# Output products of a linear-attention branch in 11 passes rather than 12, one iteration later, with other PSUM banks at two changes of pool

## The chip, the cores and the metric

The kernel runs on one core of a Trainium2 chip. The metric is device microseconds of one execution; three runs of the kernel before gave 1002.74, 1003.26 and 1003.54, median 1003.26.

## The reference

Two attentions over the same x (2048 tokens, 448 features, 16 heads of 28) are mixed by a gate per token, all in 32-bit floats:

```python
g = _sigmoid((x * gate_w).sum(-1, keepdims=True))
# A: phi = concat(softmax(pq), softmax(-pq)), pq = q @ w_phi per head
kv = einsum("bhsf,bhsd->bhfd", phi_k, v);  z = sum of phi_k over s
o  = (phi_q @ kv) / (phi_q . z + 1e-6);    a = o @ wo_A
# B: softmax(q k^T / sqrt(28)) v, then @ wo_B
return g * a + (1 - g) * b
```

## The kernel before

**Exact products.** A 32-bit product is made in three passes: every operand is a high part (rounded to the matmul's format) and a low part, and high·high, high·low and low·high are added in PSUM. The 448 features lie in four groups of 112, each as four strips of 28 rows in 32, so that 128 rows hold 112 of data. In each strip four rows are spare: row 28 carries the denominator, and the weights are zero against all four. Projections of x have 11 passes instead of 12, since x was packed so when it was loaded. The output product of branch A, `out_a` (L593), has 12: four groups times three, 128 tokens by 448 columns each, into the PSUM tile poa. Its stationary operand is oTa, its moving one woA_s.

**Order.** For TensorE (PE), VectorE (DVE), ScalarE (ACT) and GpSimd (POOL) the order of the code is the order of the engine. SyncE (SP) issues all transfers, in an order that the framework sets; an issue that waits holds up those behind it.

**The loop at L766** has 43 iterations. In the first 16 keys and values of branch A are made. After that, with y the iteration's number less 17, each one projects a tile of queries (pq, while there are any), makes features, turns them (pft, PE transposes copied out by ACT), and pushes a maximum unit `mx_unit` (L295 and after: scores of branch B in pmb and pmd, ACT's Relu into rl, two DVE reductions) between. Eight pairs of tiles go through four steps:

- even y: numerators (pn, L549), then `normalize1`: ACT copies pn to oUa, two transfers move the denominators, in four rows of oUa, into dena over 128 partitions;
- odd y: `normalize2`: DVE adds and inverts, two transfers write rda in DRAM, one broadcasts its four rows over 32 partitions each into rsa;
- even y, two pairs later: `normalize3`: DVE multiplies oUa by rsa (L430);
- odd y: `normalize4`: ACT casts the high parts into oTa (L438, two tiles), POOL subtracts for the low ones (L439, two).

`out_a(y - 10)` follows, two products a pair; `out_a2` (L601) multiplies by the gate on ACT and stores (ga to gad). Between them stand `value_b` products (pvb, 11 passes): values of branch B, copied out by ACT (L753) into vb.

**PSUM.** At q = NT + 4 (q = y + 1, NT = 16) the loop's pool closes and another opens; tiles pvb_next and poa_next are allocated ahead, so that other tiles fall on banks 2 to 7. After the loop a tail makes the remaining eight value products and the remaining maximum units, then a third pool opens (L1023) for the main loop over scores (st, L991), exponentials (p, L994), products with the values (pv, L1092) and maximum visits (pm, L332). That loop takes the larger part of the time; its qst and kst tiles are cleared by POOL ahead of it.

Of the kernel before, what the change touches and what calls it, by code (L numbers as in the profile page):

```python
# [40 lines left out]
def gated_mix_kernel(ctx, tc, xT, wqkB, wvB, wvA, wkAT, wqAT, phi, woA, woB,  # L41
# [73 lines left out]
    def run(dst, todo):  # L115
        for i, (l, r) in enumerate(todo):
            nc.tensor.matmul(dst, l, r, start=i == 0, stop=i == len(todo) - 1)  # L117
# [149 lines left out]
    rlt = ["rl", 1]  # L267

    def mx_unit():

        u = mxs["u"]
        if u == NF:
            return
        mx_fin()
        take_diffs(2)
        mxs["u"] = u + 1
        gq, r = divmod(u, 16)
        g, qb = divmod(gq, NQ)
        if gq < GM:
# [12 lines left out]
        pb, pd = ps_mx(f"pmb{u}", False), ps_mx(f"pmd{u}", True)  # L292
        for j in range(4):
            js = slice(32 * j, 32 * j + DH)
            nc.tensor.matmul((pb if j < 2 else pd)[:, j % 2, :], qc[js, qt * P:(qt + 1) * P],  # L295
                             kc[js, :], start=True, stop=True, tile_position=(32 * j, 0))
# [108 lines left out]
    def normalize1(pool, pn, nm, n):  # L405
# [4 lines left out]
        den = pool.tile([P, n, 16], F32, tag="den", name=f"den{nm}", bufs=2)  # L410
        for i in range(n):
            nc.sync.dma_start(den[:, i, :], oU[DH:P:32, i, :])
        return oU, den

    def normalize2(pool, oU, den, nm, n, eps):
# [6 lines left out]
        for k in range(n):  # L422
            nc.sync.dma_start(rd[:, k * 512:(k + 1) * 512], den[:, k, :])
        nc.sync.dma_start(rs.rearrange("p n q -> p (n q)"),
                          rd.unsqueeze(1).to_broadcast([4, 32, n * 512]))
# [7 lines left out]
    def normalize4(pool, oU, nm, n):  # L433

        oTn = []
        for k in range(n):
            oT = pool.tile([P, 2, 512], F32R, tag="oT", name=f"oT{nm}_{k}", bufs=2 * n)
            (nc.scalar.copy if n == 2 else nc.gpsimd.tensor_copy)(oT[:, 0, :], oU[:, k, :])  # L438
            nc.gpsimd.tensor_sub(oT[:, 1, :], oU[:, k, :], f32(oT[:, 0, :]))  # L439
            oTn.append(oT)  # L440
        return oTn
# [299 lines left out]
    def value_tile(i):  # L741

        pool = ctx.enter_context(tc.tile_pool(name=f"atv{i}", bufs=1, side="right", reuse_waits="tile"))
        v = pool.tile([P, NT // 2, H, 32], F32, name=f"vb{i}")
        nc.gpsimd.memset(v[:, :, :, 28:32], 0.0)
        nc.gpsimd.memset(v[:, :, :, 28:29], 1.0)
        return v
# [18 lines left out]
    for i in range(2 * NT + 11):  # L766
# [22 lines left out]
        if q == 2:  # L789
# [3 lines left out]
            KV = ta.tile([P, 512], F32, name="KV")  # L793
            kvT = kv_copy()
            early = [ta.tile([P, 2, 512], F32, tag="rl2", name=f"ve{i}", bufs=2) for i in range(2)]
# [24 lines left out]
        if q == NT + 4:  # L820
# [16 lines left out]
        if q == 3:  # L837
            kv_out(kvT)
        if 2 <= q - 1 < NT:
# [24 lines left out]
        if 0 <= y - 10 < NT:  # L864
            out_a(y - 10)
            out_a2(y - 10)
# [10 lines left out]
        if 0 <= q - NT - 2 < 5:  # L877
            value_b(q - NT + 1, (lambda i: i == 5 and mx_unit()) if q >= NT + 4 else None)
        if y >= 5 and y % 2 and tb - 2 < 8:
            num[tb - 2] = normalize2(ta, *num[tb - 2], f"a{tb - 2}", 2, True)  # L880
    ta_s.close()
# [71 lines left out]
    def score_group(sc):  # L953
# [34 lines left out]
        for (s, j), i in zip(sc, take):  # L988
            gq, kt = divmod(s, NT)
            st = bank(i, f"st{s}_{j}")  # L990
            nc.tensor.matmul(st, kst_of[(gq // NQ, kt // 4)][:, j, (kt % 4) * P:(kt % 4 + 1) * P],  # L991
# [15 lines left out]
    for t in range(8, NT):  # L1007
# [8 lines left out]
        if t in (8, 12):  # L1016
            load_k(0, t // 12)
# [67 lines left out]
    def values(s):  # L1085
        gq, kt = divmod(s, NT)
        g, qb = divmod(gq, NQ)
        if kt == 0:
# [234 lines left out]
```

## Time and profile before

| | |
|---|---|
| median of the runs | 1003.26 us |
| the profiled execution's own time | 1003.26 us |
| its span in the trace | 1001.5 us |
| TensorE clock granted | 0.999 |
| DVE busy | 659.8 us (66%) |
| ACT busy | 807.8 us (81%) |
| POOL busy | 240.0 us (24%) |

The span is what the trace covers; the profiled execution's own time is 1.76 us more. In rows of the timeline a line begins with start and duration in us, and the bracket at its end is how long the engine stood idle before it, and on whom; PEld is the loading of a matmul's stationary operand, which lies beside other matmuls.

### The profile page before, as it was taken

How to read it: one execution, taken by the hardware profiler on the slowest of the kernel's cores; microseconds unless marked ns; L12 is line 12 of the kernel's file. 1: busy time of each engine (PE TensorE's matmuls, PEld its weight loads, DVE VectorE, ACT ScalarE, POOL GpSimd, SP SyncE). 2: the span in 40 equal slices, each digit the busy share in tenths (PEclk: the TensorE clock that was granted, in tenths of full speed). 3: DMA queues.
4: the chain of work that ended last, by engine and by line, in shares of the span. 5: the costliest groups of instructions: out<-in, count | busy, mean ns of one | idle time of the engine just before them, and what ended most of it. 6: DMA issues, size and time to landing. Idle time of an engine off the chain costs nothing.

```text
span 1001.5 us, 18001 instructions
## 1 busy us (share of the span) xinstructions
PE 994.9 (99%) x6472; PEld 557.7 (56%) x6472; DVE 659.8 (66%) x1335; ACT 807.8 (81%) x1532; POOL 240.0 (24%) x222
## 2 busy tenths in 40 slices
PE   9999999999999999999999999999999999999998
PEld 8878878888777533333333333333334444455656
DVE  6467676887645588888888788888886544444202
ACT  5445555567855899999999999999999999979672
POOL 1265455678625211110120100102011011101010
PEclk9999999999999999999999999999999999999999
DMA  8977312312235832332525324443233264216231
GB/s 290 313 238 218 104 66 76 146 46 80 91 114 129 174 87 54 88 82 70 108 58 105 81 51 141 88 101 94 59 88 75 66 125 117 53 38 147 64 105 56
DMA packets 68353, 107.28 MB, mean 107 GB/s; under 512 B 18520, under 2 KB 28424, under 8 KB 68264
## 3 DMA queue, kind: packets, MB, share of 16 engines
q1 hardware_dynamic: 68264, 106.13, 39.0%
q8 instruction: 51, 0.84, 0.4%
q14 instruction: 38, 0.31, 0.1%
HBM read 73.44 MB, written 31.45 MB: 105 GB/s over the span
## 4 chain that ended last, share of the span: by engine, by line
PE 99%; DVE 0%; ACT 0%; issue 0%; POOL 0%; POOLq 0%; ACTq 0%
PE st L991 28%; PE pv L1092 25%; PE pm L332 9%; PE pqk L117 6%; PE poa L117 4%; PE pva L135 4%; PE pk L135 4%; PE pq L117 4%; PE pob L117 3%; PE pmb L295 2%; PE pvb L135 2%; PE pft L535 2%; PE pvb L117 1%; PE pqk L688 1%; PE pn L549 1%; PE pkv L489 1%
## 5 line engine op out<-in xcount | busy, mean ns | idle before, releaser
L994 ACT ACTIVATE p<-st 128x512 f32<-128x512 f32 x1020 | 527.9, 642 | 25.8 <-PE st L991 25.7
L343 DVE TENSOR_REDUCE part<-pm 128x1 f32<-128x512 f32 x450 | 287.6, 686 | 151.1 <-PE pm L332 151.1
L991 PE MATMUL st<-qst,kst 128*128 128x512 f32 x1020 | 301.3, 423 | 0.8 <-ACT vb L753 0.5
L1092 PE MATMUL pv<-p,vb 128*32 128x512 f32 x2048 | 263.6, 602 | 0.0
L991 PEld LDWEIGHTS st<-qst,kst 128*128 128x128 f32 x1020 | 168.8, 188 | 100.1 <-ACT p L994 45.0
L336 ACT ACTIVATE rl<-pm 128x512 f32<-128x512 f32 x200 | 124.7, 624 | 14.6 <-PE pm L332 13.0
L332 PEld LDWEIGHTS pm<-kc,qc 28*128 28x128 f32 x800 | 38.3, 181 | 167.7 <-issue 100.6
L430 POOL TENSOR_TENSOR oUb<-oUb,rsb 128x512 f32<-128x512 f32 x15 | 19.3, 1286 | 459.3 <-DMA rsb<-rdb 332.5
L340 DVE CUSTOM_DVE_ANT_0 rl<-pm,rl 128x512 f32<-128x512 f32 x150 | 102.2, 681 | 0.0
L332 PE MATMUL pm<-kc,qc 28*128 28x512 f32 x800 | 101.2, 495 | 0.0
L1092 PEld LDWEIGHTS pv<-p,vb 128*32 128x32 f32 x2048 | 47.4, 108 | 95.4 <-issue 88.7
L300 DVE CUSTOM_DVE_ANT_0 rl<-pmb,rl 128x512 f32<-128x512 f32 x112 | 72.1, 681 | 40.4 <-ACT rl L298 40.3
L298 ACT ACTIVATE rl<-pmd 128x1024 f32<-128x1024 f32 x56 | 57.6, 1028 | 17.0 <-PE pmd L295 9.4
L117 PE MATMUL pqk<-XH,wB 128*128 128x512 f32 x192 | 59.3, 397 | 0.0
L625 ACT CAST ev<-pqk 128x512 fp32r<-128x512 f32 x28 | 16.1, 588 | 37.9 <-PE pqk L117 28.8
L117 PE MATMUL poa<-woA_s,oTa 128*128 128x448 f32 x180 | 40.7, 375 | 0.0
L117 PEld LDWEIGHTS pqk<-XH,wB 128*128 128x128 f32 x192 | 35.4, 188 | 8.5 <-issue 1.5
L1107 DVE SCALAR_TENSOR_TENSOR acc<-pob,gate,acc 128x448 f32<-128x448 f32 x12 | 8.2, 681 | 47.1 <-PE pob L117 47.1
L135 PE MATMUL pva<-wvA_s,XH 128*128 128x450 f32 x128 | 38.6, 375 | 0.0
L135 PE MATMUL pk<-wkA_s,XH 128*128 128x448 f32 x128 | 37.5, 374 | 0.0
L626 DVE TENSOR_TENSOR ev<-pqk,ev 128x512 fp32r<-128x512 f32 x28 | 19.0, 690 | 28.0 <-ACT ev L625 27.9
L117 PE MATMUL pq<-wqA_s,XH 128*128 128x448 f32 x128 | 37.3, 374 | 0.0
(172 smaller groups left out, 1163.3 us busy)
## 6 DMA issues: line engine op xcount, KB each, us to landing
qkd<-ev SPq DMA_DIRECT2D x28, 512.0 KB
qst<-qkd SPq DMA_DIRECT2D x64, 224.0 KB
kst<-qkd SPq DMA_DIRECT2D x64, 224.0 KB
od<-oTb SPq DMA_DIRECT2D x48, 112.0 KB
rsa<-rda SPq DMA_DIRECT2D x8, 512.0 KB
rsb<-rdb SPq DMA_DIRECT2D x15, 256.0 KB
kc<-qkd SPq DMA_DIRECT2D x64, 56.0 KB
gad<-ga SPq DMA_DIRECT2D x16, 224.0 KB
```

The lines of the kernel that those rows point to most:

```text
L117: nc.tensor.matmul(dst, l, r, start=i == 0, stop=i == len(todo) - 1)
L135: nc.tensor.matmul(dst[:, :n], l, r, start=i == 0, stop=i == len(todo) - 1, skip_group_check=True)
L295: nc.tensor.matmul((pb if j < 2 else pd)[:, j % 2, :], qc[js, qt * P:(qt + 1) * P], kc[js, :], start=True, stop=True, tile_position=(32 * ...
L298: nc.scalar.activation(rl, pd, AF.Relu)
L300: nc.vector.tensor_tensor_reduce(rl[:, i, :], pb[:, i, :], rl[:, i, :], 1.0, LOWEST, ALU.add, ALU.max, part[:, col + i:col + i + 1])
L332: nc.tensor.matmul(pm[j], mxs[("qc", gq)][js, qt * P:(qt + 1) * P], mxs[("kc", g, kb)][js, :], start=True, stop=True, tile_position=(32 * ...
L336: nc.scalar.activation(rl, pm[kb], AF.Relu if kb < 3 else AF.Copy)
L340: nc.vector.tensor_tensor_reduce(r, pm[j], r, 1.0, LOWEST, ALU.add, ALU.max, part[:, col + j:col + j + 1])
L343: nc.vector.tensor_reduce(part[:, col + j:col + j + 1], pm[j], AX.X, ALU.max)
L991: nc.tensor.matmul(st, kst_of[(gq // NQ, kt // 4)][:, j, (kt % 4) * P:(kt % 4 + 1) * P], qst_of[gq][:, j, :], start=True, stop=True)
L994: nc.scalar.activation(p, st, AF.Exp, scale=SCALE)
L1092: nc.tensor.matmul(pv[32 * j:32 * j + 32, :], vb[kt // 8][:, kt % 8, 4 * g + j, :], pt[j], start=kt == 0, stop=kt == NT - 1, tile_position ...
```

## The change

**Eleven passes.** The low·high pass of the fourth group goes. Its 112 rows of the stationary operand, low parts for the pair's two tiles, are copied by four transfers per pair (`take_spread`, 28 rows to 4 spare rows times 7 slots of 256 columns, in each strip) into the spare rows of seven other passes' operands; the matching rows of the weights stand in the spare rows of the moving operands. For the low·high passes of groups 0 to 2 that takes copies of the weights: woC0, in seven strips of 64 columns that lie in unused columns of wqA_s, and woC_s. `spare_weights` loads the rows in two iterations early in the second part.

**Normalisation.** The denominators move in one transfer instead of two, the inverses in one instead of two, the broadcast in four of 32 partitions instead of one of 128. One subtraction of each pair moves from POOL to DVE. oTa is one tile a pair.

**One iteration later.** `out_a` takes y - 11, the loop has 44 iterations, five value products stand at other iterations, and one maximum unit moves from the tail into the loop (56 in all, as before). Also the rl tiles alternate between two pools near the end of the loop, and vb's ones are set later on POOL.

**PSUM.** The first change of pool comes one iteration later, without the two tiles allocated ahead: maximum units start on banks 0 to 5, others on 6 and 7. At the second change, pv0 is allocated right behind the tile st1_0.

```diff
@@ run
-            nc.tensor.matmul(dst, l, r, start=i == 0, stop=i == len(todo) - 1)
+            d = dst.rearrange("p (a n) -> p a n", n=64) if len(r.shape) == 3 else dst
+            nc.tensor.matmul(d, l, r, start=i == 0, stop=i == len(todo) - 1)
@@ mx_unit
-        rl = rlp.tile([P, 2, 512], F32, tag=rlt[0], name=f"rl{u}", bufs=rlt[1])
+        if rl_at:
+            rl_at.append(rl_at.pop(0))
+            rl = rl_at[0][0].tile([P, 2, 512], F32, tag=rl_at[0][1], name=f"rl{u}", bufs=1)
+        else:
+            rl = rlp.tile([P, 2, 512], F32, tag=rlt[0], name=f"rl{u}", bufs=rlt[1])
@@ normalize1
-        den = pool.tile([P, n, 16], F32, tag="den", name=f"den{nm}", bufs=2)
-        for i in range(n):
-            nc.sync.dma_start(den[:, i, :], oU[DH:P:32, i, :])
+        den = pool.tile([P, 16 * n], F32, tag="den", name=f"den{nm}", bufs=2)
+        nc.sync.dma_start(den, oU[DH:P:32].rearrange("p n q -> p (n q)"))
@@ normalize2
-        for k in range(n):
-            nc.sync.dma_start(rd[:, k * 512:(k + 1) * 512], den[:, k, :])
-        nc.sync.dma_start(rs.rearrange("p n q -> p (n q)"),
-                          rd.unsqueeze(1).to_broadcast([4, 32, n * 512]))
+        nc.sync.dma_start(rd, den)
+        if n == 1:
+            nc.sync.dma_start(rs[:, 0, :], rd.unsqueeze(1).to_broadcast([4, 32, 512]))
+            return oU, rs
+        for j in range(4):
+            nc.sync.dma_start(rs[32 * j:32 * j + 32].rearrange("p n q -> p (n q)"),
+                              rd[j:j + 1].to_broadcast([32, n * 512]))
@@ normalize4
-            oT = pool.tile([P, 2, 512], F32R, tag="oT", name=f"oT{nm}_{k}", bufs=2 * n)
...
-            nc.gpsimd.tensor_sub(oT[:, 1, :], oU[:, k, :], f32(oT[:, 0, :]))
+        o = pool.tile([P, n, 2, 512], F32R, tag="oT", name=f"oT{nm}", bufs=2)
...
+            (nc.vector if n == 2 and k == 0 else nc.gpsimd).tensor_sub(
+                o[:, k, 1, :], oU[:, k, :], f32(o[:, k, 0, :]))
+        if n == 2:
+            spread.append(o)
+        return [o[:, k] for k in range(n)]
+    def take_spread():
+        while spread:
+            o = f32(spread.pop())
+            for r in range(0, P, 32):
+                nc.sync.dma_start(
+                    o[r + DH:r + 32].rearrange("p k i n -> p (k i n)")[:, :1792].rearrange(
+                        "p (s n) -> p s n", n=256),
+                    o[r:r + DH, 1, 1, 256:])
+    def spare_weights(i):
+        for r in range(0, P, 32):
+            w = w_d["woA"][r:r + DH, 0, 3].rearrange("(p s) d -> p s d", s=7)
+            a, c = f32(woA_s[r + DH:r + 32, 0, :, :D]), f32(woC_s[r + DH:r + 32])
+            for d, x in (((a[:, 0:2], w[:, 0:2]), (a[:, 2:4], w[:, 4:6])) if i == 0 else
+                         ((f32(woC0[r + DH:r + 32]), w[:, 2].rearrange("p (a n) -> p a n", n=64)),
+                          (c, w[:, 3::3]))):
+                nc.sync.dma_start(d, x)
@@ out_a
-        run(po[:, :D], [x for g in range(NG)
-                        for x in out_passes(oTs[tb][g // 2], g % 2 * 256 + tl * P, woA_s[:, :, :, :D], g)])
+        todo = [x for g in range(NG)
+                for x in out_passes(oTs[tb][g // 2], g % 2 * 256 + tl * P, woA_s[:, :, :, :D], g)][:11]
+        for g in range(3):
+            todo[3 * g + 2] = todo[3 * g + 2][0], woC_s[:, g - 1, :] if g else woC0
+        run(po[:, :D], todo)
@@ the loop
-    for i in range(2 * NT + 11):
+    for i in range(2 * NT + 12):
...
+            woC_s = ta.tile([P, 2, D], F32R, name="woC_s")
+            woC0 = wqA_s.rearrange("p i b n -> p (i b) n")[:, :7, D:]
+            nc.sync.dma_start(f32(woC_s), w_d["woA"][:, 0, 1:3])
+            nc.sync.dma_start(f32(woC0), w_d["woA"][:, 0, 0].rearrange("p (a n) -> p a n", n=64))
...
-        if q == NT + 4:
+        if q == NT + 5:
...
-            pv_next.append(ps_s("pvb_next"))
-            po_next.append(ps_s("poa_next"))
         if q == NT + 8:
-            rlp, rlt[:] = ta, ("rl2", 2)
+            rl_at[:] = [(rlp, "rl"), (ta, "rl2")]
...
+            take_spread()
...
+        if q in (4, 5):
+            spare_weights(q - 4)
...
-        if 0 <= y - 10 < NT:
-            out_a(y - 10)
-            out_a2(y - 10)
+        if 0 <= y - 11 < NT:
+            out_a(y - 11)
+            out_a2(y - 11)
...
-        if 0 <= q - NT - 2 < 5:
-            value_b(q - NT + 1, (lambda i: i == 5 and mx_unit()) if q >= NT + 4 else None)
+        if q - NT in (3, 4, 6, 7, 9):
+            value_b(3 + (3, 4, 6, 7, 9).index(q - NT), (lambda i: i == 5 and mx_unit()) if q >= NT + 5 else None)
@@ scores, before the score tile's matmul
+            if (s, j) == (1, 0):
+                pv_of[0] = ps2.tile([P, 512], F32, tag="pv", name="pv0", bufs=1)
@@ set-up of the main loop
-    kst = [stack(f"kst{i}", True) for i in range(5)]
+    kst = [stack("kst0", True)]
+    value_ones(vb[1])
+    kst += [stack(f"kst{i}", True) for i in range(1, 5)]
...
+    load_k(0, 0)
```

On PE, at the first output product (names: pn numerators, pft turned features, poa output products of branch A; the figures are tile numbers), before:

```order
L549 MATMUL pn3_1_2554<-fT3_2449,KV_2053 32x256 x4
L117 MATMUL poa0_2583<-woA_s_1874,oTa0_0_2494 128x448 x6
L117 MATMUL poa0_2583<-woA_s_1874,oTa0_1_2497 128x448 x6
L535 MATMUL pft8_0_2600<-ident_76,feat0_464 128x128 x4
L535 MATMUL pft8_4_2601<-ident_76,feat0_464 128x128 x4
```

and of the change, at the same place, and then where the product stands now:

```order
L568 MATMUL pn3_0_2578<-fT3_2469,KV_2053 32x256 x4
L568 MATMUL pn3_1_2579<-fT3_2469,KV_2053 32x256 x4
L554 MATMUL pft8_0_2608<-ident_76,feat0_464 128x128 x4
L554 MATMUL pft8_4_2609<-ident_76,feat0_464 128x128 x4
L118 MATMUL pq12_2620<-wqA_s_665,XH_89 128x448 x2
```

```order
L554 MATMUL pft9_0_2663<-ident_76,feat1_465 128x128 x4
L554 MATMUL pft9_4_2664<-ident_76,feat1_465 128x128 x4
L118 MATMUL poa0_2675<-woA_s_1874,oTa0_2514 128x448 x2
L118 MATMUL poa0_2675<-wqA_s_665,oTa0_2514 128x448
L118 MATMUL poa0_2675<-woA_s_1874,oTa0_2514 128x448 x2
L118 MATMUL poa0_2675<-woC_s_2054,oTa0_2514 128x448
L118 MATMUL poa0_2675<-woA_s_1874,oTa0_2514 128x448 x2
L118 MATMUL poa0_2675<-woC_s_2054,oTa0_2514 128x448
L118 MATMUL poa0_2675<-woA_s_1874,oTa0_2514 128x448 x2
```

The product poa0 has gone from behind the fourth pair's numerators to behind the next turn, and in the third, sixth and ninth place it reads wqA_s and woC_s; it has eleven passes.

On SP, around the broadcast of the fifth pair (rsa4), before, with what each issue waits for in brackets (DMAHW and a number is an earlier transfer's end):

```order
L602 DMA gad0_69<-ga3_2840 128x448 [waits DMAHW3_49,Activation_49]
L423 DMA rda4_2845<-dena4_2737 4x32x16 [waits DMAHW4_49,DVE_49]
L423 DMA rda4_2845<-dena4_2737 4x32x16 [waits DMAHW5_49]
L424 DMA rsa4_2846<-rda4_2845 128x1x1024 [waits DMAHW6_49,DMAHW5_49,DMAHW4_49]
L412 DMA dena5_2903<-oUa5_2900 128x1x16 [waits DMAHW7_49,Activation_49]
L412 DMA dena5_2903<-oUa5_2900 128x1x16 [waits DMAHW0_49,Activation_49]
L602 DMA gad1_70<-ga4_2925 128x448 [waits DMAHW1_49,Activation_49]
L602 DMA gad1_70<-ga5_2987 128x448 [waits DMAHW2_49,Activation_49]
```

and of the change:

```order
L635 DMA gad0_69<-ga3_2937 128x448 [waits DMAHW2_49,Activation_49]
L457 DMA oTa3_2963<-oTa3_2963 4x7x256 [waits DMAHW3_49,DVE_49,Pool_49]
L431 DMA rsa4_2858<-rda4_2857 32x1024 [waits DMAHW4_49,DMAHW0_49]
L431 DMA rsa4_2858<-rda4_2857 32x1024 [waits DMAHW5_49]
L431 DMA rsa4_2858<-rda4_2857 32x1024 [waits DMAHW6_49]
L431 DMA rsa4_2858<-rda4_2857 32x1024 [waits DMAHW7_49]
L457 DMA oTa3_2963<-oTa3_2963 4x7x256
L457 DMA oTa3_2963<-oTa3_2963 4x7x256 [waits DMAHW1_49]
L457 DMA oTa3_2963<-oTa3_2963 4x7x256 [waits DMAHW2_49]
L635 DMA gad1_70<-ga4_3001 128x448 [waits DMAHW3_49,Activation_49]
```

The broadcast is four issues now and stands behind the first of the four spread transfers of the fourth pair (oTa3), whose wait for DVE and POOL is ahead of it; the other three follow it.

On PE, at the first change of PSUM (pvb and pvb_next value products of branch B, pmb and pmd the maximum unit), before:

```order
L117 MATMUL pvb4_3192<-wvB_s_1875,XL_90 128x448
L117 MATMUL pvb4_3192<-wvB_s_1875,XH_89 128x448 x2
L295 MATMUL pmb37_3211<-kp0_1_520,qp2_0_1524 128x512 x2
L295 MATMUL pmd37_3212<-kp0_1_520,qp2_0_1524 128x512 x2
L117 MATMUL poa_next_3210<-woA_s_1874,oTa4_0_3073 128x448 x6
L117 MATMUL poa_next_3210<-woA_s_1874,oTa4_1_3076 128x448 x6
```

and of the change:

```order
L118 MATMUL pvb4_3242<-wvB_s_1875,XL_90 128x448
L118 MATMUL pvb4_3242<-wvB_s_1875,XH_89 128x448 x2
L296 MATMUL pmb38_3268<-kp0_1_520,qp2_0_1524 128x512 x2
L296 MATMUL pmd38_3269<-kp0_1_520,qp2_0_1524 128x512 x2
L118 MATMUL poa9_3279<-woA_s_1874,oTa4_3087 128x448 x2
L118 MATMUL poa9_3279<-wqA_s_665,oTa4_3087 128x448
L118 MATMUL poa9_3279<-woA_s_1874,oTa4_3087 128x448 x2
L118 MATMUL poa9_3279<-woC_s_2054,oTa4_3087 128x448
L118 MATMUL poa9_3279<-woA_s_1874,oTa4_3087 128x448 x2
L118 MATMUL poa9_3279<-woC_s_2054,oTa4_3087 128x448
L118 MATMUL poa9_3279<-woA_s_1874,oTa4_3087 128x448 x2
L296 MATMUL pmb39_3294<-kp0_1_520,qp2_0_1524 128x512 x2
```

Before, the first unit on new banks is pmb37, behind the value product pvb4 and ahead of poa_next; now it is pmb38, in the same place, and poa9 and another unit follow.

More of the change, by code (lines that the diff above doesn't have):

```diff
@@ L433, in normalize4 @@
     def normalize4(pool, oU, nm, n):
-        oTn = []
+        o = pool.tile([P, n, 2, 512], F32R, tag="oT", name=f"oT{nm}", bufs=2)
         for k in range(n):
-            oT = pool.tile([P, 2, 512], F32R, tag="oT", name=f"oT{nm}_{k}", bufs=2 * n)
[L438 to L441, printed above, removed]
+            (nc.scalar.copy if n == 2 else nc.gpsimd.tensor_copy)(o[:, k, 0, :], oU[:, k, :])
+            (nc.vector if n == 2 and k == 0 else nc.gpsimd).tensor_sub(
[3 more added lines that the diff above has]
+        return [o[:, k] for k in range(n)]
+    spread = []
+    def take_spread():
[6 more added lines that the diff above has]
+                    o[r:r + DH, 1, 1, 256:])
     def out_passes(oT, c, w, g):
@@ L793, in gated_mix_kernel @@
             KV = ta.tile([P, 512], F32, name="KV")
+            woC_s = ta.tile([P, 2, D], F32R, name="woC_s")
+            woC0 = wqA_s.rearrange("p i b n -> p (i b) n")[:, :7, D:]
+            nc.sync.dma_start(f32(woC_s), w_d["woA"][:, 0, 1:3])
+            nc.sync.dma_start(f32(woC0), w_d["woA"][:, 0, 0].rearrange("p (a n) -> p a n", n=64))
             kvT = kv_copy()
-            early = [ta.tile([P, 2, 512], F32, tag="rl2", name=f"ve{i}", bufs=2) for i in range(2)]
+            early = [ta.tile([P, 2 - i, 512], F32, tag=f"rl{i + 2}", name=f"ve{i}", bufs=1) for i in range(2)]
             early = [e.rearrange("p t (h d) -> p t h d", d=32) for e in early]
@@ L1015, in gated_mix_kernel @@
         take_acts()
-        if t in (8, 12):
-            load_k(0, t // 12)
+        if t == 12:
+            load_k(0, 1)
     while mxs["u"] < NF:
@@ L1087, in values @@
         g, qb = divmod(gq, NQ)
-        if kt == 0:
+        if kt == 0 and gq:
             pv_of[gq] = ps2.tile([P, 512], F32, tag="pv", name=f"pv{gq}", bufs=1)
```

8 lines of the change are left out of this document (6 added, 2 removed).

## The prediction

> **What bounds the kernel now.** The first view is the page's head and its chain of work.
>
> ```profile
> span 1001.5 us, 18001 instructions
> ...
> PE 994.9 (99%) x6472; PEld 557.7 (56%) x6472; DVE 659.8 (66%) x1335; ACT 807.8 (81%) x1532; POOL 240.0 (24%) x222
> ...
> PE 99%; DVE 0%; ACT 0%; issue 0%; POOL 0%; POOLq 0%; ACTq 0%
> ```
>
> PE is busy for 994.9 of 1001.5 us, and 99% of the chain that ended last is PE's. So the end is set by how much PE has to do and by the few places where it stops. The second view, the waits of PE, names every one of these places; the last three columns are the total, the count and the longest.
>
> ```profile
> PE pqk L671 <- POOL ident masks.py:199: 1.4, 1, 1.4
> PE pmb L295 <- ACT vb L753: 0.6, 1, 0.6
> PE st L991 <- ACT vb L753: 0.5, 1, 0.5
> PE st L991 <- DVE acc L1107: 0.3, 1, 0.3
> ```
>
> The middle two belong to the change: each is the first matmul on PSUM banks that were handed over. Everything else that PE could gain is work taken out of its stream. So the sum has three terms: passes removed, stalls removed, and stalls added, chiefly the wait of an output product for the new spread transfers.
>
> **The passes removed.** The third view is the chain in order of time (start, duration).
>
> ```profile
> 212.02 2.23 PE pq L117 x11
> ...
> 240.93 2.66 PE poa L117 x12
> ...
> 248.16 2.46 PE poa L117 x12
> ```
>
> An output product of 12 passes takes 2.46 us where it follows work of the same form; the 2.66 of the other contains 0.2 of drain after the narrow numerator matmuls, which the change doesn't touch. That is 2.46/12 = 0.205 us a pass, and 2.23/11 = 0.203 in the projection of queries beside it. I take 0.204. Each of the 16 products loses one: 16 × 0.204 = **−3.27 us**. All of it lies on PE, which has no slack there, so it comes off the chain in full, unless PE then waits.
>
> The eleven passes that stay keep their shape (448 output columns, 128 rows). One of them per product reads its moving operand as seven strips of 64 columns from spare columns of another weight tile. No row of the trace has a moving operand in strips. Bounds: nothing, since as many elements are read in the same order, and at worst a second pass each, 16 × 0.204 = +3.3. I take nothing, by the rows nearest to it (passes from 0.203 to 0.205 whatever weight tile they read), and keep the other end as a rival. Strips that read faster than a contiguous row I exclude, so there is no gain below nothing.
>
> **The two stalls removed.**
>
> ```profile
> 279.96 0.50 PE L295 MATMUL pmb<-kp,qp 28*128 28x512 f32 x2 [0.62 <-ACT vb L753]
> ```
> ```profile
> 279.37 0.53 ACT L753 COPY vb<-pvb 128x448 f32<-128x448 f32 x1 [1.05 <-PE pvb L117]
> ```
>
> At the first change of PSUM the maximum unit follows a value product at once, and its bank is the one that ACT is just copying out: the copy runs from 279.37 to 279.90 and PE starts 0.06 later. In the order of the changed kernel the first unit after the change takes banks 0 and 1 (no longer 2 to 5), which were freed an iteration earlier; the bank of the value product just made goes to the next unit, with a 2.2 us output product in between. **−0.62 us**, and nothing is late next there: ACT's copy takes 0.53, the product ahead of the next unit 2.2.
>
> ```profile
> 335.53 0.73 PE L991 MATMUL st<-qst,kst 128*128 128x512 f32 x2 [0.48 <-ACT vb L753]
> 336.20 1.07 PE L1092 MATMUL pv<-p,vb 128*32 128x512 f32 x8
> ```
> ```profile
> 333.01 2.05 ACT L950 ACTIVATE p<-st 128x1024 f32<-128x1024 f32 x2 [0.23 <-PE st L942]
> 334.96 0.53 ACT L753 COPY vb<-pvb 128x448 f32<-128x448 f32 x1
> ```
>
> At the second change the second score tile waits for the copy of the last value product, which ends at 335.49. In the changed order the bank of that product is not among the next score tiles'; the value accumulator, allocated earlier, takes a bank whose exponential is the second of the two at 333.01, over by 335.06, before PE reaches that accumulator (at 336.20, or 335.72 without the stall). **−0.48 us**, kept only if ACT follows; see the rivals.
>
> **The stall added.** Now a product of the first tile of a pair cannot start before four spread transfers of that pair have landed. Tightest is the pair whose casts are at 259.42; its first product takes the place of the one at 267.99.
>
> ```profile
> 257.80 0.50 PE L295 MATMUL pmb<-kp,qp 28*128 28x512 f32 x2
> ...
> 267.99 2.70 PE L117 MATMUL poa<-woA_s,oTa 128*128 128x448 f32 x12
> ```
> ```profile
> 259.42 1.16 ACT L438 CAST oTa<-oUa 128x512 fp32r<-128x512 f32 x2
> ...
> 268.37 1.17 ACT L438 CAST oTa<-oUa 128x512 fp32r<-128x512 f32 x2
> ```
> ```profile
> 260.53 2.54 POOL L439 TENSOR_TENSOR oTa<-oUa,oTa 128x512 fp32r<-128x512 f32 x2
> ```
> ```profile
> 239.40 1.16 SPq L423 DMA_DIRECT2D rda<-dena  x2
> 242.02 0.55 SPq L424 DMA_DIRECT2D rsa<-rda  x1
> ```
>
> Counted from 257.80: the casts end at +2.78; POOL now makes one subtraction of 2.54/2 = 1.27, to +4.05 (the other is on DVE meanwhile); then SP issues eight transfers, because the four broadcasts of the next pair stand between the first spread and the other three. One issue takes about 0.54 (0.55 in the last row), so the eighth starts at 4.05 + 7 × 0.54 = +7.83. The product is due at 267.99 − 257.80 = 10.19, less two passes already saved, 0.41: +9.78. That leaves 1.95 us for ℓ, the time from the start of the last issue to landing. The other pairs by the same steps: 5.1, 5.9, 3.7, then this 1.95, then 2.1 plus what was waited before it, 2.65, 3.8 plus what was waited, 3.1.
>
> What is ℓ? Nearest are the two SP rows: a small transfer with a dependent one behind it. The second of the two at 239.40 starts near 239.98, and the broadcast that needs it at 242.02: 2.04 us for 8 KB. A spread moves 28 KB, from four partitions at a time. The row nearest in rate is the broadcast out of four rows (columns: stretch, length, then PE, PEld, DVE, ACT, POOL busy, clock, share of the DMA engines, GB/s):
>
> ```profile
> 210.50:215.50 5.00, 5.00 (x30) 4.66 (x29) 4.20 (x9) 2.88 (x5) 3.97 (x3) 1.00 0.25 91
> ```
>
> A share of 0.25 is 4 of 16 engines, 91 GB/s: 28.7 KB take 0.3. So ℓ ≈ 2.3 and the tightest pair waits 0.35; the others wait nothing. I take **+0.4 us**. The bounds: 0 (ℓ below 1.95) and, with ℓ = 6.8 as in a row of the slower rival below, 4.85 at this pair alone. The Trainium skill has a rule that speaks against cutting the broadcast into four ("DMA: Bandwidth & Descriptors", Rules for kernel authors: two transfers to disjoint partition halves serialize, so one should be used); the same page, under "Why a DMA increments its semaphore by 16 and not by 1", makes the number of engines a divisor of the slowest dimension, which would give 4 engines to a transfer out of 4 rows and 16 to one of 32 rows. The 0.25 above agrees with the second rule; by the first the four would last the old 5 us together and the spreads behind them would land at about 4.6 + 5.0 + 0.9 = +10.5, a wait of 0.7 rather than 0.4.
>
> **The rest costs nothing**, each for a reason. DVE takes the subtraction over:
>
> ```profile
> L626 DVE TENSOR_TENSOR ev<-pqk,ev 128x512 fp32r<-128x512 f32 x28 | 19.0, 690 | 28.0 <-ACT ev L625 27.9
> ```
> ```profile
> 261.47 1.09 DVE L469 TENSOR_REDUCE fsumq<-feat 128x32 f32<-128x896 f32 x1 [0.57 <-ACT feat L462]
> ...
> 276.90 1.23 DVE L430 TENSOR_TENSOR oUa<-oUa,rsa 128x1024 f32<-128x1024 f32 x1 [1.04 <-DMA rsa<-rda]
> ```
>
> 0.69 a pair, into waits of DVE for ACT and transfers of 0.57 to 1.04 (that cover gone, 8 × 0.69 on DVE, and PE would see it only through the maximum units). The broadcast now issues behind a spread that waits for the subtraction, so DVE's multiplication may start up to 0.6 later, inside the 1.04; behind the waiting spread stand on SP that broadcast and the gate store, which ACT needs two iterations later. SP gains five issues a pair; twelve in all are 6.5 us of the 9.0 between the two casts above. The 18 loads of weights stand some 60 us ahead of their use. The products one iteration later shift PE's work, not its amount.
>
> **Sum**, against the profiled execution, whose own time is 1003.26 (1.76 around the span), the same as the median of the runs: 1003.26 − 3.27 − 0.62 − 0.48 + 0.4 = **999.3 us**.
>
> **Rivals.**
>
> *Slower: the spreads land late.* All small transfers share one queue with stores and the broadcasts, and the trace has slow ones:
>
> ```profile
> 267.86 0.53 SPq L424 DMA_DIRECT2D rsa<-rda  x1
> ...
> 270.85 1.24 SPq L423 DMA_DIRECT2D rda<-dena  x2
> ...
> 278.27 0.55 SPq L424 DMA_DIRECT2D rsa<-rda  x1
> ```
>
> Three microseconds behind a broadcast, the second small transfer starts at 271.47 and its dependant at 278.27: up to 6.8 us. At ℓ = 3 the pairs wait 1.05 + 0.35 = 1.4 (1000.3); at 3.9 about 4.2, all that was gained; above 4.45 more than 6.4, and the kernel is over 2 us slower; at 5 it is 1.3 + 3.05 + 2.35 + 1.9 = 8.6 (1007.5). For it: this row. Against it: what held those transfers up was a broadcast confined to a quarter of the engines, which the change cuts up.
>
> *Strips cost a second pass:* 999.3 + 3.3 = 1002.6. Nothing speaks for it but that no row shows the form.
>
> *The gain isn't passed on*, since ACT is nearly as full as PE in the main loop (PE, PEld, DVE, ACT, POOL):
>
> ```profile
> 350.00:400.00 50.00, 50.00 (x313) 19.23 (x310) 40.26 (x83) 48.38 (x98) 8.43 (x8) 1.00 0.30 70
> ```
>
> 48.38 of 50 us: PE arriving earlier finds ACT with 3% of room, and the 0.48 of the second stall may come back as a wait for an exponential: 999.8. Against more than that: ACT's own inputs come earlier by as much as PE does.
>
> **Chances.** Forecast (ℓ up to 3, 998.9 to 1000.3) 0.70; larger ℓ up to 3.9 0.08; slower by late spreads 0.08; strips 0.07; gain given back at ACT 0.07. The range runs from 998.4 (no wait, with half a microsecond for what the shifted order may save) to 1002.6 (strips) and leaves out the late spreads. A measurement of this kernel can tell about 0.2%, 2 us, from no change: faster 0.70 + 0.07 + half of the 0.08 = 0.81; within 2 us 0.11; slower 0.08.
>
> **What would show it.** Eleven passes in 2.25 and 2.45 us in the chain (strips: above 2.4 and 2.6); the two waits for ACT's copy gone from PE's list; a new wait of a product for a transfer, at the fourth pair, under 1 us. Waits there of 3 us, or waits for DVE's subtraction or for exponentials right after the second change, would make this wrong.

## The result, and the profile after

The changed kernel takes 1007.38 us (median of six runs, 1006.88 to 1009.51) beside 1003.68 for the kernel before (six runs, 1002.74 to 1004.75): a ratio of 1.0039, 95% interval 1.0026 to 1.0052. It is 3.7 us slower, where 4 us faster was forecast. Later comparisons are each with runs of the kernel before on the same chip, whose median lay between 1002.58 and 1003.13.

The page of the changed kernel:

```profile
span 1005.5 us, 18087 instructions
...
PE 993.6 (99%) x6456; PEld 555.5 (55%) x6456; DVE 670.0 (67%) x1343; ACT 807.4 (80%) x1532; POOL 230.8 (23%) x214
...
PE 95%; SPq 1%; DMA 1%; DVE 1%; ACT 0%; issue 0%; POOL 0%; POOLq 0%; ACTq 0%; DVEq 0%
```

PE has sixteen matmuls fewer, as it should, and yet the span is 4.0 us longer. The chain that ended last is no longer PE's alone: SP's issues, transfers and DVE are in it. The waits of PE say where:

```profile
PE poa L118 <- DMA oTa<-oTa: 3.7, 2, 2.4
PE poa L118 <- DMA gad<-ga: 1.9, 1, 1.9
PE pqk L704 <- POOL ident masks.py:199: 1.4, 1, 1.4
PE poa L118 <- ACT rl L303: 0.6, 2, 0.4
PE st L1036 <- DVE acc L1155: 0.3, 1, 0.3
PE poa L118 <- ACT vb L790: 0.3, 1, 0.3
```

The two waits for ACT's copy at the changes of PSUM (0.62 and 0.48) are gone. In their place stand six waits of output products, 6.5 us in all. The one put down to a gate store ("gad<-ga", 1.9) is a wait for spreads too: that store was issued 0.1 us behind the last spread of its pair, and the product doesn't read what it writes. So, most likely, are those put down to ACT (0.17, 0.40 and 0.29): each of these products starts 3.5 to 3.7 us after the last spread of its pair began to be issued, as the others do (3.4 to 3.6), and without spreads (e1, below) none of the waits is there. For the 0.17 alone the end of ACT's Relu would fit as well. The chain in order of time shows the passes themselves:

```profile
238.90 2.44 PE poa L118 x11
245.91 2.24 PE poa L118 x11
```

2.24 for eleven passes, 0.204 each, against 2.46 for twelve; the strips cost nothing. At the longest stop, though, a product is slow as well. The timeline of PE, and below it the windows around that stop (PE, PEld, DVE, ACT, POOL busy, granted clock, DMA share, GB/s):

```profile
284.52 0.50 PE L296 MATMUL pmb<-kp,qp 28*128 28x512 f32 x2
...
287.39 1.09 PE L118 MATMUL poa<-woA_s,oTa 128*128 128x448 f32 x2 [2.36 <-DMA oTa<-oTa]
288.65 0.95 PE L118 MATMUL poa<-woA_s,oTa 128*128 128x448 f32 x2
```
```profile
284.90:287.00 2.10, 0.13 (x4) 0.00 (x0) 1.65 (x4) 2.10 (x4) 0.00 (x0) 1.00 0.58 186
287.00:290.50 3.50, 3.11 (x9) 2.82 (x10) 2.10 (x3) 0.20 (x1) 1.34 (x3) 0.51 0.09 33
290.50:292.00 1.50, 1.50 (x9) 1.31 (x7) 0.00 (x0) 0.64 (x1) 0.00 (x0) 1.00 0.61 188
```

After 2.36 us without work the granted clock is 0.51 for 3.5 us; the product takes 3.88 in the chain instead of 2.44 as the next one does, 1.4 us more:

```profile
287.39 3.88 PE poa L118 x11
...
294.57 2.44 PE poa L118 x11
```

So the stops cost 6.5 + 1.4 = 7.9 in this trace.

Now the pair that the prediction took for the tightest, on SP and DVE of the changed kernel:

```profile
259.93 0.64 SPq L457 DMA_DIRECT2D oTa<-oTa  x1
260.67 2.07 SPq L431 DMA_DIRECT2D rsa<-rda  x4
262.78 1.98 SPq L457 DMA_DIRECT2D oTa<-oTa  x3
264.86 0.39 SPq L635 DMA_DIRECT2D gad<-ga  x1
```
```profile
258.11 1.76 DVE L445 TENSOR_TENSOR oTa<-oUa,oTa 128x512 fp32r<-128x512 f32 x1
```
```profile
258.03 1.29 POOL L445 TENSOR_TENSOR oTa<-oUa,oTa 128x512 fp32r<-128x512 f32 x1
```
```profile
267.65 0.64 PE L118 MATMUL poa<-woA_s,oTa 128*128 128x448 f32 x2 [1.93 <-DMA gad<-ga]
```

DVE's subtraction lasts until 259.87, 0.55 behind POOL's; the eight issues start over 4.2 us; the last spread starts at 262.78 + 1.98 - 0.64 = 264.12 and its product at 267.65: a landing of 3.5 us. Here and below, landing is counted from the start of the pair's last issue to the start of the product that waited for it.

### The profile page after: what moved, and what is told of

Same layout as the page of the kernel before. It is cut to its first block, busy times and chain, and to the rows that moved or that the text cites. A ratio compares the mean times of both kernels' runs of the same rounds, so it can differ in the third digit from the quotient of the medians.

```text
span 1005.5 us, 18087 instructions
## 1 busy us (share of the span) xinstructions
PE 993.6 (99%) x6456; PEld 555.5 (55%) x6456; DVE 670.0 (67%) x1343; ACT 807.4 (80%) x1532; POOL 230.8 (23%) x214
## 4 chain that ended last, share of the span: by engine, by line
PE 95%; SPq 1%; DMA 1%; DVE 1%; ACT 0%; issue 0%; POOL 0%; POOLq 0%; ACTq 0%; DVEq 0%
PE st L1036 28%; PE pv L1140 25%; PE pm L337 9%; PE pqk L118 6%; PE pva L136 4%; PE pk L136 4%; PE pq L118 4%; PE pob L118 3%; PE pvb L136 2%; PE poa L118 2%; PE pmb L296 2%; PE pft L554 1%; PE pqk L721 1%; PE pkv L508 1%; PE poL L1178 1%; SPq L457 1%
```

## The experiments

Theory L says that the loss is PE's stops for late spread transfers, and the rest of the sum was right. Theory S, its rival, puts the loss on the strips, the shift by an iteration or the banks.

**No spread transfers** (e1).

```diff
-            take_spread()
+            spread.clear()
```

> Leaves out the four spread transfers of every pair (the spare rows then hold other data, so the low-by-high part of the fourth group is not added); the eleven passes, the shift by one iteration and the banks stay. Theory L (late spreads): PE's stops ahead of the output products 6, 8, 10 and 14 (1.93, 0.29, 2.36 and 1.31 us) and the lowered clock behind the longest (about 1.3 us) go: 1007.4 - 7.2 = about 1000.2, and PE waits for no transfer. Rival S (strips, the shift or the banks cost): those stay, and it remains above 1004.

Measured 998.12 beside 1002.58, ratio 0.9953 (0.9938 to 0.9967): 4.5 us under the kernel before, where passes and stalls alone were reckoned at 4.37. PE's list keeps two waits only:

```profile
PE pqk L704 <- POOL ident masks.py:199: 1.4, 1, 1.4
PE st L1036 <- DVE acc L1155: 0.3, 1, 0.3
```

Theory S falls. The main loop's first product with values starts at 331.32 here and at 340.27 in the change, 8.9 us later. Of these 0.34 stood already before the first spread was issued (the numerators ahead of it start at 226.40 and 226.74). The stops and the clock explain 7.9; the rest, 0.7 in small slips, is not assigned.

**Twelve passes, no spreads** (e8): also without spare weights.

```diff
-                for x in out_passes(oTs[tb][g // 2], g % 2 * 256 + tl * P, woA_s[:, :, :, :D], g)][:11]
-        for g in range(3):
-            todo[3 * g + 2] = todo[3 * g + 2][0], woC_s[:, g - 1, :] if g else woC0
+                for x in out_passes(oTs[tb][g // 2], g % 2 * 256 + tl * P, woA_s[:, :, :, :D], g)]
...
-            take_spread()
+            spread.clear()
...
-        if q in (4, 5):
-            spare_weights(q - 4)
```

> Twelve passes again, no spread transfers and no loads of spare weights; the shift by one iteration, the merged and split transfers of the normalisation, the subtraction on DVE and the banks stay. Theory L: the time of the kernel without spreads plus 16 x 0.204 = 3.3, so about 1003.5, 0.3 to 1 below the kernel before, whose two stalls at PSUM changes (0.62 and 0.48) are gone. Rival S: the shift or the banks cost something, above 1005.

1001.37 beside 1002.58, ratio 0.9987 (0.9977 to 0.9996): 1.2 us faster than the kernel before, by the two stalls at PSUM (1.1). The difference to e1, 3.25, is 16 × 0.203. This is the fastest version here that does the whole computation; it beats both kernels.

**A quarter of the bytes** (e2): each spread moves 64 of 256 columns.

```diff
-                        "p (s n) -> p s n", n=256),
-                    o[r:r + DH, 1, 1, 256:])
+                        "p (s n) -> p s n", n=256)[:, :, :64],
+                    o[r:r + DH, 1, 1, 256:320])
```

> Each spread moves 64 of its 256 columns (7 KB rather than 28; the rest of the spare rows keeps other data, so part of the low-by-high product of the fourth group is wrong). If the landing of a spread is paid by its bytes, it falls from 3.4 us after the last issue to about 2.3 and PE's stops shrink by 3 us or more (below 1004.5). If it is a fixed time (theory L's form), the landing stays above 3.0 and the time within 1 us of the change's.

998.86 in one run. The last pair's fourth spread starts at 299.84 (the first of these rows, less one issue) and the product at 301.91: landing in 2.07 us.

```profile
297.70 2.78 SPq L457 DMA_DIRECT2D oTa<-oTa  x4
```
```profile
301.91 0.64 PE L118 MATMUL poa<-woA_s,oTa 128*128 128x448 f32 x2 [0.60 <-DMA oTa<-oTa]
```

So fewer bytes go with a shorter landing. But the framework also ordered SP otherwise here, with the spreads of most pairs in one row, so that this run alone doesn't separate bytes from order.

**Both subtractions on POOL** (e4).

```diff
-            (nc.vector if n == 2 and k == 0 else nc.gpsimd).tensor_sub(
+            nc.gpsimd.tensor_sub(
```

> Both subtractions of a pair on POOL again, one after the other (2.55 us), none on DVE. In the change the two run side by side and last up to 1.7 us. Theory L: the first spread of a pair is issued about 0.7 us later, the stops of PE grow, +0.5 to +2.5 us. Rival D (the place on DVE behind two reductions is what makes the spreads late): the spreads are issued earlier, and the time falls by 1 us or more.

1008.22 in one run beside 1002.58, 5.6 over the kernel before against 3.7 for the change; stops of 9.6 us against 6.5, though no lowered clock follows any of them. The moved subtraction helps, as theory L has it; its place on DVE is not the fault.

**Stores later, from ACT** (e10): gate stores out of the way of the spreads.

```diff
-        nc.sync.dma_start(ga_d[t // 4][:, t % 4], ga)
+        ga_late.append((t, ga))
+        if t:
+            store_ga()
...
+    def store_ga():
+        t, ga = ga_late.pop(0)
+        nc.scalar.dma_start(ga_d[t // 4][:, t % 4], ga)
```

> The gate stores (224 KB, 16 engines) are issued by ACT, each one product later, instead of by SP right behind the spread transfers. Theory C (the last spread lands late because a gate store issued behind it runs on the same engines, and because stores stand ahead of spreads on SP): landing after the last issue falls from 3.4 to 3.6 us to about 2.6, the stops ahead of products 6, 10 and 14 from 1.9, 2.4 and 1.3 to about 1.1, 0.6 and 0.4, the clock is not lowered: about 1002.5, 4 to 5 us under the change. Rival O (the spread's own 28 KB out of 28 rows by four engines take that long): landing stays at 3.2 or more and the time within 1.5 us of the change's 1007.4.

1009.98 beside 1003.05, ratio 1.0056 (1.0035 to 1.0076). Three stops make 6.4 us, and the landing is 3.7 to 4.1 us: nothing gained. In the trace the clock is at half behind each of the three; the one run of the four whose mean granted clock was 1.000 took 1006.25, the others, at 0.995, 1009.63 to 1010.80. It doesn't refute theory C cleanly, since the stores came to lie among the spreads again, only from another queue:

```profile
306.08 2.80 SPq L457 DMA_DIRECT2D oTa<-oTa  x4
```
```profile
307.33 0.33 ACTq L643 DMA_DIRECT2D gad<-ga  x1
```
```profile
312.09 0.64 PE L118 MATMUL poa<-woA_s,oTa 128*128 128x448 f32 x2 [1.56 <-DMA oTa<-oTa]
```

At this last pair the fourth spread starts near 308.23, the windows show data until 310.3, and the product starts at 312.09. What holds it for the last 1.8 us no view shows.

**Casts at the end of the iteration before** (e12): the block with `normalize4` and `take_spread` stands behind `out_a2`, at even y from 8.

```diff
-        if y >= 9 and y % 2 and tb - 4 < 8:
+        if y >= 8 and y % 2 == 0 and tb - 4 < 8:
```

> The casts, subtractions and spreads of a pair stand at the end of the iteration before (behind the output product and its gate, ahead of a value product), two to four microseconds earlier. Theory L: PE's stops ahead of the output products (1.9, 0.3, 2.4, 1.3 us and the lowered clock's 1.3) go but for 0.5 us: about 1000.5 on the scale of the change's 1007.4, 2.5 to 4 us under the kernel before. Rival A: ACT's cast waits for DVE's multiplication and so for a late broadcast, holds up the score and gate copies behind it, and gives back 2 us or more (above 1002.5).

1009.58 beside 1003.05, ratio 1.0065 (1.0050 to 1.0080). No product waits for a spread any more, and it is slower still: rival A. ACT's cast now waits for DVE's multiplication, and what is queued behind it on ACT stops PE, twice with the clock at half behind the stop:

```profile
PE pft L554 <- ACT fT L557: 4.6, 2, 3.0
PE poa L118 <- ACT fT L557: 1.5, 1, 1.5
```

**Casts ahead of the maximum unit** (e3): the same block, above `mx_unit()` of its own iteration.

```diff
-        if q in (0, 1) or q >= 11:
-            mx_unit()
         if y >= 9 and y % 2 and tb - 4 < 8:
...
+        if q in (0, 1) or q >= 11:
+            mx_unit()
```

> Casts, subtractions and spreads stand ahead of the maximum unit of their iteration instead of behind it: ACT casts 1.0 us earlier, DVE subtracts ahead of its two reductions. Theory L: the first spread of a pair is issued about 1 us earlier, the stops at products 6 and 14 shrink by about 1 us each, that at 10 by less since SP still waits for a gate store there: -2 to -4 us against the change. Rival: nothing, since SP and not the subtraction sets the issue.

1003.74 in one run beside 1003.05, some 3 us better than the change. Left are a stop of 2.5 at product 6, with the lowered clock behind it, and two of 0.6 and 0.4. At product 6 four broadcasts still stand among the spreads and took 3.25 us to issue.

**One broadcast again** (e5).

```diff
...
-        for j in range(4):
-            nc.sync.dma_start(rs[32 * j:32 * j + 32].rearrange("p n q -> p (n q)"),
-                              rd[j:j + 1].to_broadcast([32, n * 512]))
+        nc.sync.dma_start(rs.rearrange("p n q -> p (n q)"),
+                          rd.unsqueeze(1).to_broadcast([4, 32, n * 512]))
```

> The broadcast is one transfer of 128 partitions out of four rows again, three issues fewer on SP. If four transfers of 32 partitions use more engines than one out of four rows, the single one lasts about 5 us at a share of 0.25 of the engines, the spreads queued behind it land 2 us or more later, and the kernel is slower than the change by 3 us or more. If they serialize anyway, it is faster by about 1 us at the pairs where a broadcast stands between the spreads (three issues of 0.45 us fewer).

1028.02 in one run beside 1003.05: 20 us slower than the change.

```profile
PE poa L118 <- DMA oTa<-oTa: 13.1, 3, 6.8
PE poa L118 <- ACT oTa L440: 4.1, 1, 4.1
PE poa L118 <- DMA dena<-oUa: 3.6, 1, 3.6
```

Here is the landing of many microseconds behind a broadcast that the prediction's slower rival feared. The split into four is what keeps it away. The Trainium skill's advice against two transfers to disjoint partitions ("DMA: Bandwidth & Descriptors", Rules for kernel authors) does not hold for a broadcast out of four rows; the same page's rule on the number of engines agrees, with a DMA share of 0.25 for the one broadcast of the kernel before and 0.91 where the four move in the changed kernel (262.50 to 263.50).

**Only the order on SP** (e14): broadcasts of the next pair ahead of all four spreads.

```diff
...
+            with tc.issue_after(rsa_last[0].ins):
                 for r in range(0, P, 32):
                     nc.sync.dma_start(
```

> Only the order on SP changes: the four broadcasts of the next pair stand ahead of the four spread transfers of this pair (in the change they stand behind the first of them). Theory Q (part of the lateness is SP's order): the last spread of the pair of casts near 257 is issued at about 262 rather than 264.1, its stop of 1.93 us goes; the pairs without broadcasts in between keep theirs (2.36 with the lowered clock, 1.3): about 2 us under the change, 1005.4. Rival F (the four engines are the limit, not the issue): the spreads land as late as before, within 0.7 us of the change.

1003.30 beside 1003.13, ratio 1.0003 (0.9993 to 1.0012): 3.5 us of the change's loss, more than the 2 that were expected. The pair of the rows above issues its spreads from 259.37 to 262.01, and its product stops for 0.46 instead of 1.93. What stays is the stop at product 10 (1.86) with the clock behind it, and one of 1.28 at product 14.

**Order and casts** (e15): e14 and e3 together.

> Casts ahead of the maximum unit and broadcasts ahead of the spreads together. Theory L with Q: stops of PE for spreads under 0.7 us in all, no lowered clock: 999 to 1000.5, 2.5 to 4 us under the kernel before. Rival F: the stop at product 6 stays at 2 us or more with the lowered clock behind it, about 1003.5 as with the casts first alone.

1002.86 beside 1003.13, ratio 0.9997 (0.9988 to 1.0006), no difference. The trace is of a run of 1004.80, one of two out of eleven that took over 1004; both had a mean granted clock of 0.998, the others 0.999 or 1.000. In it the stop at 6 is gone, but one of 1.74 appears at product 12: the last spread of that pair was issued at 292.00 and its wait ended at 296.86, with copies into vb, loads and a store beside it (DMA share about 1.0 from 294.5 on). The clock is at half behind it. Two smaller stops are 0.73, of a maximum unit for DVE, and 0.32 at product 10.

**One strip** (e16): one spread a pair instead of four.

```diff
-            for r in range(0, P, 32):
+            for r in range(96, P, 32):
```

> One spread per pair (the last strip) instead of four; the spare rows of the other strips keep other data. If a spread of 28 KB takes 3.4 us to land by itself, its landing stays at 3.2 or more after its issue. If the four queue for the same four engines (each holds them for 0.5 to 0.75 us and one is issued every 0.65), a single one lands in 2.4 to 2.8. The time falls to 998 to 999 in either case.

999.10 in one run, and no stop. The single spread of the last pair is issued at 297.79; the windows show next to nothing from 298.25 to 299, then its packets, then a store:

```profile
298.25:299.00 0.75, 0.75 (x6) 0.69 (x5) 0.73 (x4) 0.03 (x1) 0.00 (x0) 1.00 0.01 2
299.00:300.25 1.25, 1.25 (x9) 0.73 (x7) 0.00 (x0) 0.60 (x1) 0.00 (x0) 1.00 0.13 34
300.25:301.25 1.00, 1.00 (x9) 0.88 (x6) 0.00 (x0) 0.77 (x1) 0.00 (x0) 1.00 0.62 229
```

Its data moves from 1.2 to 2.5 us after issue. No product waits for it, so its landing as counted here is not measured. In e10 the windows show data until 2.1 us after the issue of the fourth spread, and the product still started 1.8 later. So this run does not show that a spread alone lands sooner than the fourth of four. The changed kernel's windows at its last pair don't either; there the spreads start at 304.50 to 306.65, a store is issued at 307.40, and the product starts at 310.26:

```profile
305.75:307.00 1.25, 1.25 (x9) 0.69 (x7) 0.00 (x0) 0.56 (x1) 0.00 (x0) 1.00 0.20 57
307.00:307.25 0.25, 0.25 (x5) 0.23 (x2) 0.00 (x0) 0.06 (x1) 0.00 (x0) 1.00 0.00 0
307.25:308.25 1.00, 1.00 (x6) 0.82 (x5) 0.00 (x1) 0.96 (x1) 0.00 (x0) 1.00 0.19 52
308.25:309.00 0.75, 0.70 (x6) 0.19 (x4) 0.75 (x3) 0.46 (x1) 0.00 (x0) 1.00 0.92 279
309.00:310.00 1.00, 0.00 (x0) 0.00 (x0) 0.56 (x2) 1.00 (x2) 0.00 (x0) 1.00 0.09 25
```

The spreads keep a fifth of the engines busy, with a gap at 307.00; the store's burst follows at 308.25, and whose data moves in the last microsecond cannot be told. Whether the last spread waits for its sisters, for the store or for neither stays open.

**Halves** (e17): e14, with four spreads of 14 KB for the pair's first tile and four for the second.

```diff
...
+                for h in range(0, 256, P):
                     for r in range(0, P, 32):
...
+                                "p (s n) -> p s n", n=256)[:, :, h:h + P],
+                            o[r:r + DH, 1, 1, 256 + h:256 + h + P])
```

> Broadcasts ahead of the spreads as before, and each spread in two of 14 KB: four for the pair's first tile, then four for its second, which is wanted an iteration later. Theory F' (the spreads of a pair queue for the same few engines, so landing goes by the bytes ahead): the first four land about 2.6 us after the last of them is issued rather than 3.4 to 3.6, the stop at product 10 falls from 1.9 to about 1 and the one at 14 below 0.5; 1001 to 1002, 1.5 to 2.5 us under the order alone (1003.3). Rival I (each issue and its landing are a fixed time): landing stays, and four more issues on SP make it 1003.5 or more.

1008.37 beside 1002.64, ratio 1.0052 (1.0036 to 1.0068). Both theories had a part: the landing does fall, to 2.5 us at product 10,

```profile
284.92 5.30 SPq L459 DMA_DIRECT2D oTa<-oTa  x8
```
```profile
289.39 0.79 PE L118 MATMUL poa<-woA_s,oTa 128*128 128x448 f32 x2 [4.29 <-DMA oTa<-oTa]
```

(the fourth of eight starts at 284.92 + 3 × 0.67 = 286.93), but eight issues hold SP for 5.3 us, and the inverses and broadcasts behind them push the next pair's spreads back. SP's row of issues is itself a limit.

**Halves and casts** (e19).

> Halved spreads, broadcasts ahead of them, and casts ahead of the maximum unit. With F' and the earlier casts the stops for spreads are below 0.5 us in all and the clock isn't lowered: 999.5 to 1001, 2 to 3.5 us under the kernel before. If the stop of 1.7 us at product 12, behind the large copies into vb, is set by those copies, it stays, with the lowered clock: about 1002.

1009.66 beside 1002.64, ratio 1.0067 (1.0054 to 1.0080); a miss for the same reason.

**Two of four on POOL** (e18, and timed again): e14, with two spreads on POOL's queue.

```diff
-                    nc.sync.dma_start(
+                    (nc.sync if r < 64 else nc.gpsimd).dma_start(
```

> Broadcasts ahead of the spreads, and two of the four spreads issued by POOL instead of SP. If issue in a row on one queue is what counts, the last of SP's is issued 1.3 us earlier and the stops at 10 and 14 shrink by about 1 us each: 1001 to 1002. If POOL takes longer to start a transfer, or all share the same engines, there is no gain: 1003 or more.

> The kernel with two of four spreads on POOL and the broadcasts ahead, timed: its one look gave 1002.34 beside 1002.64 of the kernel before. Its stops for spreads (0.7), for the maximum units and the numerators (1.5) are 2.2 us over the sum without spreads (998.1 to 998.9): 1000.5 to 1002.5.

A single run gave 1002.34; timed, 1002.80 beside 1002.76, ratio 0.9999 (0.9990 to 1.0007). The stops for spreads are down to 1.0 us, but two new ones stand at one iteration, with 3.4 us at half clock behind them (the single run has the same two without it):

```profile
259.35 0.50 PE L296 MATMUL pmd<-kp,qp 28*128 28x512 f32 x2 [0.68 <-DVE part L305]
260.62 1.16 PE L569 MATMUL pn<-fT,KV 56*32 56x256 f32 x32 [0.77 <-ACT fT L558]
```

DVE is late there because a multiplication that takes 1.16 in the change takes 3.29 beside POOL's:

```profile
254.78 3.29 DVE L437 TENSOR_TENSOR oUa<-oUa,rsa 128x1024 f32<-128x1024 f32 x1
```

**All four on POOL** (e20).

```diff
-                    nc.sync.dma_start(
+                    nc.gpsimd.dma_start(
```

> All four spreads issued by POOL, right behind its own subtraction; SP keeps stores, inverses and broadcasts only. Theory: SP's row of issues and the lateness of the broadcasts go; POOL's fourth is issued as late as SP's fourth was (0.61 each), so landing and the stops at 10 and 14 stay near 1 us; 1001 to 1003. Rival (the POOL queue uses other or more engines): no stop for a spread, below 1000.5.

1011.37 beside 1002.76, ratio 1.0083 (1.0069 to 1.0097). Stops for spreads are 3.2 us, and the multiplications on DVE now take up to 5.07.

## Why the prediction was wrong, step by step

- Passes removed (-3.27): right. Without spreads, eleven passes beat twelve by 3.25 us (e1 against e8).
- Stalls removed (-0.62 and -0.48): right. They are gone from PE's list, and e8 is 1.2 us under the kernel before.
- Strips at nothing: right, 2.24 us for eleven passes.
- The gain passed on by ACT in the main loop: right, e1 shows the whole 4.5 us at the end.
- **The stall added (+0.4): wrong by 7.5 us**, and it is the step that failed: "So ℓ ≈ 2.3 and the tightest pair waits 0.35; the others wait nothing." Measured were stops of 6.5 us at six products and 1.4 us of lowered clock. In its parts, at the tightest pair, counted from the same maximum unit (255.09 in the changed kernel): the casts ended at +2.78, as reckoned. The subtractions ended at +4.78, not +4.05. The eighth issue started at +9.03, not +7.83 (a spread takes 0.64 to issue, not 0.54). Landing took 3.5, not 2.3. That sums to 2.4 us, of which 0.35 + 2.4 less 0.85 by which the product itself was due later gives the 1.9 that was measured. At this pair the landing is the largest part. The price was taken from one small transfer with nothing behind it; the last of four of 28 KB, issued 0.65 apart, landed after 3.4 to 3.6 us, of four of 14 KB after 2.5 (e17), of four of 7 KB after 2.07 (e2). Why the larger ones take that long is open.
- The landing alone does not make the loss. With 3.5 for ℓ and the prediction's own times for the rest, the waits come to about 2.8 us; 6.5 were measured. The time that the prediction left for the landing was too long at every pair that stopped: 3.55, 3.1, 1.6, 3.2, 1.0 and 2.3 (landing less stop, at products 0, 4, 6, 8, 10 and 14), where 5.1, 3.7, 1.95, 2.1 and the 1.93 waited before it, 2.65 and 3.1 had been reckoned.
- "The others wait nothing" failed by what stands ahead on SP: at product 10 the spreads were issued 0.9 us after the subtraction, behind broadcasts, a load and a store, and stopped PE for 2.36, longer than the pair taken for the tightest.
- "DVE takes the subtraction over" at 0.69: mis-sized. The row used has one operand from PSUM; this one reads two from SBUF beside POOL, and takes up to 1.76.
- The slower rival had the right mechanism and the right side, with a chance of 0.08. It put the point of decision at ℓ = 4.45; with the later subtraction and issue and the clock, 3.5 was enough. What spoke against it (the split broadcast) was true, as e5 shows, and not sufficient. Its price at ℓ = 3.9, "all that was gained", left out the clock.

The experiments settle that the spreads are the whole loss, and that SP's order (e14) and the time of the subtraction (e4, one run) each hold a part of it; that the bytes of a spread do is supported by e17 and e2, with other things changed beside them. They do not settle what makes the landing long, the sisters of a spread or other traffic: moving the stores (e10) only moved where they meet the spreads, and at product 12 of e15 a spread with much traffic beside it landed after 4.9 us.

## What to carry to other kernels

When a change puts a transfer between two engines' work, price the whole path to its landing at the busiest place: the last of several issues on its queue, behind everything else the queue must issue, with what else is in flight. Here a slack of 2 us against a landing reckoned at 2.3 was not a small stop but the largest term. On a kernel bound by PE a stop of two microseconds can have a lowered clock behind it (1.4 us more at one stop here, nothing at others as long), so it is priced as a range; and a fallback without the transfer (e8) belongs among the first things tried.

## What the hardware showed that was not expected

- **The clock after a stop.** The granted clock fell to 0.5 for about 3.4 us behind stops of 2.36 (the change), 1.86 (e14), 1.74 (e15) and of 0.68 and 0.77 in one iteration (e18 timed). It did not fall behind 1.93 at 267.65 in the change, nor behind 2.88 and 2.36 in e4, nor behind 0.69 and 0.77 in the single run of e18, which is the same kernel. So the length of a stop alone does not decide it here, and it differs between runs of one kernel (e10, e15). The Trainium skill ("TensorE: Matmul & The Clock Gate", What's actually happening) has the drop after an idle window of about 3.4 us; the length of the slow stretch agrees, but far shorter stops were enough here. The page also says that the window runs free, which could do it, and no run here shows the window.
- **DVE beside POOL.** The subtraction takes 0.69 on DVE or 1.28 on POOL where the other is done or idle; side by side one of the two is stretched, DVE to 1.76 or POOL to 1.74, and a multiplication of DVE from 1.16 to as much as 5.07 (e20). The Trainium skill ("SBUF — State Buffer", SBUF: two separate sides) describes a port pair that one of them locks for a whole instruction if DVE reads two operands from SBUF; in the change DVE's subtraction ends 0.55 behind POOL's in all four pairs where POOL began first, which is near that; a full 0.69 behind would fit better.
